# A cross-attention and maxout kernel: its opening re-ordered, and its two PSUM pools joined into one ring

## The chip, the cores and the metric

The kernel runs on one core of one Trainium2 chip. The metric is the device time of one execution in microseconds (us). The kernel before takes 152.98 us, the median of three runs (152.91 to 153.26). The profiled execution took 152.91 us by that measure; its trace spans 151.1 us from the first to the last instruction, so a time is about 1.8 us more than the span of its trace. The granted TensorE clock is 1.00 throughout.

Engines are named as the profile names them: PE is TensorE (PEld its weight loads), DVE is VectorE, ACT is ScalarE, POOL is GpSimd, and SP is the engine that issues the DMAs.

## The reference

Eight batches of 8 heads. Tokens `x` (512 per batch and head, 64 wide) and a small `state` (32 rows per head) attend to each other; both reads then go, as rows of 512 features, through a maxout layer.

```python
# B, H, S, Ns, D = 8, 8, 512, 32, 64
scores = scale * x @ state^T ;   a  = softmax(scores)     # over the 32 states
xread  = a @ state                                        # 512 rows per head
scores2 = scale * state @ x^T ;  a2 = softmax(scores2)    # over the 512 tokens
sread  = a2 @ x                                           # 32 rows per head
rows   = concat([xread, sread])                           # (8*544, 512)
out    = max(rows @ w1, rows @ w2) @ w_out                # w1, w2: 512x1024, w_out: 1024x512
```

Inputs and output are float32. The kernel works in bf16 on PE and rests on an identity: max(h1, h2) = h2 + relu(h1 - h2), so out = relu(rows @ (w1 - w2)) @ w_out + rows @ (w2 @ w_out). The weight W = [w1 - w2 | w2 @ w_out], 512 x 1536, is called `wcat`. For the x rows, a @ (state @ W) is used in place of (a @ state) @ W: `SW[b]` is state times W for batch b, in three column parts (0 and 1 for the relu, 2 for the direct part).

## The kernel before

The program is one hand-ordered list: each engine runs its own instructions in the order of the text. First the loads are issued on one DMA queue:

```python
load_states(first)                  # states of batches 0 to 2
load_x(0, 2)                        # x of batch 0, in two DMAs (even heads, odd heads)
for ch in range(2):
    load_w(w2f, moe_w2, ch)         # half of w2, 1 MB
    load_wo(2 * ch); load_wo(2 * ch + 1)   # two quarters of w_out, 0.5 MB each
load_w(w1f, moe_w1, 0)
load_x(1)
load_w(w1f, moe_w1, 1)
load_states(slice(3, 8))
load_x(2)
```

The pieces that both versions are made of (cut):

```python
def d_xt(b):        # x of a batch, transposed by a DMA from the bf16 copy xc
    nc.sync.dma_start_transpose(out=st[b]["xt"], in_=st[b]["xc"]...)
def u_exp(b, g):    # scores of half the heads (16 small matmuls in all for g = 0, 1), then exp on ACT
def u_norm(b, g, mul):   # row sums and reciprocal on DVE, then a = e * er on the engine `mul`
def u_sr(b):        # state read: 32 small matmuls, then reciprocal and scaling on DVE
def u_at(b, eng):   # a transposed by PE (8 transposes), copied out by `eng`
def compact_x(b, g, eng="A"):   # half of x cast to bf16 into xc
def w_sub(q, eng=nc.gpsimd):    # a quarter of w1 - w2 into wcat
    eng.tensor_sub(wcat[:, :, cs], w1f[:, :, cs], w2f[:, :, cs])
def w_wo(q, i): ... # w2 @ w_out, 2 of the 8 terms of row block i

def sw_mm(b, ch, engs="VA"):        # SW[b], column part ch, 8 matmuls on two PSUM banks
    pg = [bank(kind="acc" if ch == 2 and b > 1 else "ps") for g in range(2)]
    two = b < TWO and ch == 0       # from w1 and -w2 apart (16 matmuls), as wcat isn't there yet
    terms = ((sbd, w1b), (sneg, w2b)) if two else ((sbd, wcat),)
    ...                             # copied out: one bank by DVE, one by ACT

def l1(b, fill, fs=range(NF), engs=None):    # 8 blocks of 2 matmuls and a relu, ACT and DVE in turn
def l2_open(b, c): ...   # 2 matmuls of the direct part open the sum of output block c (4 blocks)
def l2_add(b, c, fs):    # one matmul for each f in fs onto the sum of block c
def l2_close(b, c): ...  # copied out by DVE (c even) or ACT (c odd)
```

PSUM has eight banks, four in a pool `ps` and four in a pool `acc`. The opening, from the second half of w_out on:

```python
    ...                                   # x(0) transposed, scored; w2 transposed; w2 @ w_out begun
    for e, i in (("V", slice(0, 2)), ("A", slice(2, 3)), ("P", slice(3, 4))):
        copy(e, w1b[:, i, 0:512], w1f[:, i, 0:512])       # first half of w1 to bf16, three engines
    for i in range(4):
        w_wo(3, i)
    w_wo_out(0); w_wo_out(1)
    u_sw(0, 0)
    w_wo_out(2); w_wo_out(3)
    compact_x(1, 0, "P"); compact_x(1, 1, "P")
    d_xt(1)
    l1(0, {2: [lambda: u_sw(0, 2)]}, range(0, 4))
    cast_x(1, (("A", slice(0, 4)), ("A", slice(4, 8))))
    load_x(3)
    w_sub(2, nc.vector); w_sub(3, nc.vector)
    cast_states("P", rest)
    sT = d_states(rest)
    for c in range(NC):
        l2_open(0, c)
    for c in range(NC - 1):
        l2_add(0, c, range(0, 4))
    u_sw(0, 1)
    l2_add(0, 3, range(0, 4))
    u_exp(1, 0); u_exp(1, 1)              # needs xt(1)
    l1(0, {}, range(4, 8))
    u_norm(1, 0, nc.vector); u_norm(1, 1, nc.gpsimd)
    cast_x(2)
    w_sub(0); w_sub(1)
    l2_add(0, 0, range(4, 8)); l2_close(0, 0)
    u_sw(1, 1)
    u_sr(1)
    l2_add(0, 1, range(4, 8)); l2_close(0, 1)
    u_sw(1, 0)
    compact_x(2, 0); compact_x(2, 1)
    d_xt(2)
    l2_add(0, 2, range(4, 8)); l2_close(0, 2)
    u_at(1, "V")
    u_sw(1, 2)
    u_srt(1)
    l2_add(0, 3, range(4, 8)); l2_close(0, 3)
    l2_out(0)
    for b in range(1, B):                 # the main loop, seven batches
        fill = fillers(b)                 # the next batch's scores, state read, DMAs and SW, set
        ...                               # between the blocks of l1(b) and l2(b)
        l1(b, fill)
        if b == B - 1:
            moe_sread()                   # the state rows through the maxout layer
        l2(b, fill)
```

Of the kernel before, what the change touches and what calls it, by code (L numbers as in the profile page):

```python
# [9 lines left out]
BF16 = mybir.dt.bfloat16  # L10
# [5 lines left out]
def kernel(  # L16
# [14 lines left out]
    nc = tc.nc  # L31
# [4 lines left out]
    FF = moe_w1.shape[1]  # L36
# [11 lines left out]
    keep = ctx.enter_context(tc.tile_pool(name="keep", bufs=2))  # L48
    big = ctx.enter_context(tc.tile_pool(name="big", bufs=2))

    pools = {k: ctx.enter_context(tc.tile_pool(name=k, bufs=4, space=bass.MemoryType.PSUM)) for k in ("ps", "acc")}
    ctx.enter_context(tc.manual_schedule())

    def bank(dtype=F32, kind="ps"):
        return pools[kind].tile([128, 512 if dtype == F32 else 1024], dtype, tag="b", name=kind)

    def acc():
        return bank(kind="acc")

    def copy(eng, o, i):  # L60
        if eng == "A":
            nc.scalar.copy(o, i)  # L62
        elif eng == "V":
            nc.vector.tensor_copy(o, i)  # L64
        else:
            nc.gpsimd.tensor_copy(o, i)  # L66
# [11 lines left out]
    def load_x(b, parts=1):  # L78
        xf_t[b] = xio.tile([128, H, NC * D], F32, tag="xf", name="xf")
        for g in range(parts):  # L80
            nc.sync.dma_start(out=xf_t[b][:, g::parts, :], in_=x[b, g::parts].rearrange("h (p c) d -> p h (c d)", c=NC))  # L81
# [12 lines left out]
    def load_w(t, w, ch):  # L94
        cs = slice(ch * 512, (ch + 1) * 512)
        nc.sync.dma_start(out=t[:, :, cs], in_=w.rearrange("(i p) f -> p i f", p=128)[:, :, cs])  # L96
# [3 lines left out]
                          in_=moe_w_out.rearrange("(k p) n -> p k n", p=128)[:, 2 * q:2 * q + 2])  # L100

    load_states(first)
    load_x(0, 2)
    for ch in range(2):
        load_w(w2f, moe_w2, ch)
        load_wo(2 * ch)
        load_wo(2 * ch + 1)
    load_w(w1f, moe_w1, 0)
    load_x(1)
    load_w(w1f, moe_w1, 1)  # L110
    load_states(slice(3, 8))
    load_x(2)

# [6 lines left out]
    sneg = consts.tile([128, TWO, 4, Ns], BF16)  # L120
    wo = consts.tile([128, NF, DM], BF16)
    wcat = consts.tile([128, 4, WC], BF16)
    w1b = stage.tile([128, 4, 512], BF16)
    w2b = stage.tile([128, 4, FF], BF16)
    w2t = stage.tile([128, 4, NF, 128], BF16)

    def warm_up(n):
        p = bank()
        for k in range(n):
            nc.tensor.matmul(p, warm[:, 0:128], warm, start=(k == 0), stop=(k == n - 1))  # L130
# [28 lines left out]
    def negate_states():  # L159
        for g in range(2):  # L160
            gs = slice(64 * g, 64 * g + 64)
            negate("V", sneg[gs], sbd[gs, 0:TWO, g::2, g, :])
# [11 lines left out]
    def cast_x(b, parts=(("P", slice(0, 8)),)):  # L174
        new_x(b)
        xp = st[b]["xp"] = xio.tile([128, H, NC, 66], BF16, tag="xp", name="xp")
        nc.gpsimd.memset(xp[:, :, :, 64:65], 1.0)
        for e, hs in parts:
            copy(e, xp[:, hs, :, 0:64], xf_t[b][:, hs].rearrange("p h (c d) -> p h c d", c=NC))
# [40 lines left out]
    def u_norm(b, g, mul):  # L220
        d = st[b]
        nc.vector.tensor_reduce(d["es"][:, g], d["e"][:, g].rearrange("p i c n -> p (i c) n"),  # L222
                                axis=mybir.AxisListType.X, op=ALU.add)
        nc.vector.reciprocal(d["er"][:, g], d["es"][:, g])  # L224
        mul.tensor_mul(  # L225
            d["a"][:, g].rearrange("p c i n -> p i c n"), d["e"][:, g],
            d["er"][:, g].rearrange("p (i c) -> p i c", i=4).unsqueeze(3).to_broadcast([128, 4, NC, Ns]))
# [22 lines left out]
    def u_at(b, eng):  # L250
        d = st[b]
        AT[b] = keep.tile([128, 2, NC * 128], BF16, tag="at", name="aT")
        p = bank(BF16)
        for g in range(2):
            for c in range(NC):
                nc.tensor.transpose(p[:, (g * NC + c) * 128:(g * NC + c + 1) * 128],
                                    d["a"][:, g, c].rearrange("p i n -> p (i n)"), ident)
        copy(eng, AT[b].rearrange("p g t -> p (g t)"), p)
# [8 lines left out]
    swt = consts.tile([128, 2, 2, WC], BF16)  # L267

    def sw_mm(b, ch, engs="VA"):

        pg = [bank(kind="acc" if ch == 2 and b > 1 else "ps") for g in range(2)]
        two = b < TWO and ch == 0
        terms = ((sbd, w1b), (sneg, w2b)) if two else ((sbd, wcat),)
        for k, (sv, w) in enumerate(terms):
            for i in range(4):
                for g in range(2):
                    gs = slice(64 * g, 64 * g + 64)
                    nc.tensor.matmul(pg[g][32 * i:32 * i + 32, :],  # L278
                                     sneg[gs, b, i, :] if k else sbd[gs, b, 2 * i + g, g, :],
                                     w[gs, i, ch * 512:(ch + 1) * 512],  # L280
                                     start=(k == 0), stop=(k == len(terms) - 1))
        return lambda: [copy(engs[g], SW[b][:, g, ch * 512:(ch + 1) * 512], pg[g]) for g in range(2)]
# [96 lines left out]
                nc.sync.dma_start(out=out[b * L + S:(b + 1) * L], in_=ob[32 * q:32 * q + 32, t, :])  # L379


    def w_sub(q, eng=nc.gpsimd):
        cs = slice(q * 256, (q + 1) * 256)
        eng.tensor_sub(wcat[:, :, cs], w1f[:, :, cs], w2f[:, :, cs])

    def w_cast(o, w, ch, engs="VA"):
        cs = slice(ch * 512, (ch + 1) * 512)
        for k in range(2):
            copy(engs[k], o[:, 2 * k:2 * k + 2, cs], w[:, 2 * k:2 * k + 2, cs])
# [4 lines left out]
    def w_t(ch, half, eng):  # L394
        p = bank(BF16)
        for j in range(2):
            for k in range(4):
                f = 4 * ch + k
                nc.tensor.transpose(p[:, (4 * j + k) * 128:(4 * j + k + 1) * 128],
                                    w2b[:, 2 * half + j, f * 128:(f + 1) * 128], ident)  # L400
        copy(eng, w2t[:, 2 * half:2 * half + 2, 4 * ch:4 * ch + 4, :].rearrange("p j f t -> p j (f t)"),
             p.rearrange("p (j t) -> p j t", j=2))
# [3 lines left out]
    def w_wo(q, i):  # L406
        if q == 0:
            WO[i] = acc()
        for f in range(2 * q, 2 * q + 2):
            nc.tensor.matmul(WO[i], w2t[:, i, f, :], wo[:, f, :], start=(f == 0), stop=(f == NF - 1))  # L410

    def w_wo_out(i):
        copy("V" if i % 2 else "A", wcat[:, i, FF:WC], WO[i])


    def fillers(b):
# [22 lines left out]
    warm_up(6)  # L439
    cast_states("V", first)  # L440
    states(first)
    warm_up(9)
    cast_x(0, (("A", slice(0, 4, 2)), ("V", slice(4, 8, 2)), ("P", slice(1, 4, 2)), ("V", slice(5, 8, 2))))
    u_xt(0, 0, "V")
    warm_up(2)
    u_xt(0, 1, "A")
    u_exp(0, 0)
    warm_up(2)
    u_exp(0, 1)
    warm_up(3)  # L450
    w_cast(w2b, w2f, 0, "PA")
    u_norm(0, 0, nc.vector)
    u_norm(0, 1, nc.vector)
    w_t(0, 0, "A")
    w_t(0, 1, "A")
    u_sr(0)
    wo_cast(0, "P")
    wo_cast(1, "P")
    warm_up(1)
    for i in range(4):  # L460
        w_wo(0, i)
    u_at(0, "V")
    w_cast(w2b, w2f, 1)
    for i in range(4):
        w_wo(1, i)
    w_t(1, 0, "V")
    w_t(1, 1, "A")
    negate_states()
    wo_cast(2, "P")
    wo_cast(3, "P")  # L470
    u_srt(0)
    warm_up(2)
    for i in range(4):
        w_wo(2, i)
    for e, i in (("V", slice(0, 2)), ("A", slice(2, 3)), ("P", slice(3, 4))):
        copy(e, w1b[:, i, 0:512], w1f[:, i, 0:512])
    for i in range(4):
        w_wo(3, i)
    w_wo_out(0)
    w_wo_out(1)  # L480
    u_sw(0, 0)
    w_wo_out(2)
    w_wo_out(3)
    compact_x(1, 0, "P")
    compact_x(1, 1, "P")
    d_xt(1)
    l1(0, {2: [lambda: u_sw(0, 2)]}, range(0, 4))
    cast_x(1, (("A", slice(0, 4)), ("A", slice(4, 8))))
    load_x(3)
    w_sub(2, nc.vector)  # L490
    w_sub(3, nc.vector)
    cast_states("P", rest)
    sT = d_states(rest)
    for c in range(NC):
        l2_open(0, c)
    for c in range(NC - 1):
        l2_add(0, c, range(0, 4))
    u_sw(0, 1)
    l2_add(0, 3, range(0, 4))
    u_exp(1, 0)  # L500
    u_exp(1, 1)
    l1(0, {}, range(4, 8))
    u_norm(1, 0, nc.vector)
    u_norm(1, 1, nc.gpsimd)
    cast_x(2)
    w_sub(0)
    w_sub(1)
    l2_add(0, 0, range(4, 8))
    l2_close(0, 0)
    u_sw(1, 1)  # L510
    u_sr(1)
    l2_add(0, 1, range(4, 8))
    l2_close(0, 1)
    u_sw(1, 0)
    compact_x(2, 0)
    compact_x(2, 1)
    d_xt(2)
    l2_add(0, 2, range(4, 8))
    l2_close(0, 2)
    u_at(1, "V")  # L520
    u_sw(1, 2)
    u_srt(1)
    l2_add(0, 3, range(4, 8))
    l2_close(0, 3)
    l2_out(0)
    for b in range(1, B):
        fill = fillers(b)
        if b + 2 < B:
            cast_x(b + 2)
            if b + 3 < B:  # L530
                load_x(b + 3)
        if b == 1:
            fill[11].append(lambda: put_states(rest, sT))
        l1(b, fill)
        if b == B - 1:
            moe_sread()
        l2(b, fill)
# [30 lines left out]
```

## Time and profile before

| What | Value |
|---|---|
| Time, median of three | 152.98 us |
| Span of the trace | 151.1 us |
| Instructions | 3008 |
| Matmul 128x512 of the output sums (L321), mean | 379 ns each as recorded, issued one each 0.216 us |
| DMA, whole span | 29.89 MB, mean 198 GB/s |
| HBM read, written | 15.20 MB, 8.91 MB |

The trace has three parts. The opening reaches from the start to the first matmul of the main loop, which stands at 42.77 us on the timeline. The main loop then takes one batch after the other. The end holds the state rows and the last batch's output. In a view of the timeline a row gives the start in us, the busy time in us, the engine, the line of the program, the operation, the tile written and the tiles read, the shape, and how many instructions are merged in the row; in brackets is the idle time of the engine ahead of it and what ended it. Line 64 is the copy of DVE, line 62 that of ACT and line 66 that of POOL, so these are told apart by their tiles. In the chain of waits a row gives a start, a length, and what filled it.

### The profile page before, as it was taken

What the parts mean: (1) busy time and instruction counts of PE and PEld (TensorE: products, weight loads), DVE (VectorE), ACT (ScalarE), POOL (GpSimd) and SP (SyncE); (2) the same over time, 40 slices, a digit from 0 to 9 for tenths busy, and PEclk for the clock granted to TensorE, in tenths of its full rate; (3) what the DMA queues carried; (4) which work ended last, traced back from release to release, by engine and by line L of the source; (5) the groups of instructions that cost most, each with busy time, mean ns of one, the idle gap of its engine ahead of it and who ended that gap; (6) DMA issues with size and microseconds to landing.
All of it is one profiled execution on the core that took longest, in us unless ns stands there. A gap on an engine that the chain in (4) does not pass through costs nothing.

```text
span 151.1 us, 3008 instructions
## 1 busy us (share of the span) xinstructions
PE 140.4 (93%) x1237; PEld 67.3 (45%) x1257; DVE 82.7 (55%) x149; ACT 74.8 (49%) x126; POOL 42.9 (28%) x46
## 2 busy tenths in 40 slices
PE   6979897979999999999999999999999999999991
PEld 1445542424444434544543454345445444664460
DVE  5548636815987367806762584558167726631120
ACT  3166536615888347815863684469157126621010
POOL 3145255410599540370054007303200500000000
PEclk9999999999999999999999999999999999999999
DMA  4999999999269995975888397952496030602423
GB/s 100 382 385 387 386 359 348 319 143 288 52 117 306 313 177 195 295 168 112 262 293 167 95 292 241 165 193 104 86 129 278 0 74 22 256 0 68 138 98 119
DMA packets 37950, 29.89 MB, mean 198 GB/s; under 512 B 24880, under 2 KB 33328, under 8 KB 37040
## 3 DMA queue, kind: packets, MB, share of 16 engines
q1 hardware_dynamic: 37792, 29.56, 70.7%
q8 instruction: 10, 0.16, 0.4%
q10 hardware_dynamic: 144, 0.13, 0.3%
q14 instruction: 4, 0.03, 0.1%
HBM read 15.20 MB, written 8.91 MB: 160 GB/s over the span
## 4 chain that ended last, share of the span: by engine, by line
PE 68%; DMA 13%; SPq 11%; DVE 4%; issue 1%; ACT 0%
PE acc L321 31%; PE ps L306 15%; PE acc L317 8%; DMA xt<-xc 7%; SPq L96 7%; DMA s_f<-in_state_dram 6%; PE ps L215 2%; SPq L81 2%; PE ps L365 2%; PE acc L375 2%; PE ps L278 2%; SPq L99 2%; PE ps L238 1%; PE acc L355 1%; PE acc L373 1%
## 5 line engine op out<-in xcount | busy, mean ns | idle before, releaser
L321 PE MATMUL acc<-wo,r 128*128 128x512 bf16 x239 | 58.5, 379 | 0.7 <-issue 0.2
L321 PEld LDWEIGHTS <-r 128*128 128x128 bf16 x248 | 24.0, 98 | 29.6 <-issue 0.6
L296 DVE TENSOR_SCALAR r<-ps 128x512 bf16<-128x512 f32 x32 | 22.1, 691 | 15.6 <-PE ps L306 15.6
L306 PE MATMUL ps<-aT,swt 128*128 128x512 bf16 x127 | 29.2, 379 | 0.9 <-DVE swt L64 0.8
L225 POOL TENSOR_TENSOR a<-e,er 128x512 bf16<-128x512 bf16 x13 | 13.4, 1048 | 55.5 <-DVE er L224 28.3
L64 DVE COPY ob<-acc 128x512 f32<-128x512 f32 (+1 forms) x17 | 11.1, 652 | 30.2 <-PE acc L321 29.8
L62 ACT COPY ob<-acc 128x512 f32<-128x512 f32 (+1 forms) x16 | 9.2, 573 | 28.5 <-PE acc L321 20.9
L294 ACT ACTIVATE r<-ps 128x512 bf16<-128x512 f32 x32 | 19.2, 601 | 5.2 <-PE ps L306 4.5
L306 PEld LDWEIGHTS <-swt 128*128 128x128 bf16 x128 | 12.1, 98 | 15.4 <-DVE swt L64 1.2
L62 ACT CAST swt<-ps 128x512 bf16<-128x512 f32 x18 | 10.0, 587 | 17.1 <-PE ps L278 17.1
L317 PE MATMUL acc<-swt,aT 128*128 128x512 bf16 x56 | 16.7, 380 | 1.2 <-issue 1.0
L66 POOL CAST xp<-xf 128x2048 bf16<-128x2048 f32 (+1 forms) x7 | 12.2, 1743 | 9.3 <-DMA xf<-in_x_dram 9.3
L64 DVE CAST swt<-ps 128x512 bf16<-128x512 f32 x18 | 11.8, 682 | 2.6 <-PE ps L278 2.5
L222 DVE TENSOR_REDUCE es<-e 128x16 f32<-128x512 bf16 x16 | 10.6, 662 | 3.7 <-ACT e L218 3.7
L62 ACT CAST xc<-xf 128x1024 bf16<-128x1024 f32 x12 | 12.0, 1051 | 0.0
L218 ACT ACTIVATE e<-ps 128x512 bf16<-128x512 f32 x16 | 8.8, 595 | 2.9 <-PE ps L215 2.2
L130 PE MATMUL ps<-warm 128*128 128x512 bf16 x24 | 7.6, 443 | 1.3 <-POOL warm L116 1.3
L410 PE MATMUL acc<-wo,w2t 128*128 128x512 bf16 x30 | 7.3, 379 | 0.5 <-POOL wo L66 0.4
L317 PEld LDWEIGHTS <-aT 128*128 128x128 bf16 x62 | 4.7, 98 | 6.4 <-issue 3.1
L215 PE MATMUL ps<-sbd,xt 128*128 128x64 bf16 x128 | 5.2, 193 | 1.8 <-DMA xt<-xc 1.1
L215 PEld LDWEIGHTS <-xt 128*128 128x128 bf16 x128 | 4.6, 98 | 4.3 <-DMA xt<-xc 2.2
L66 POOL CAST wo<-wof 128x1024 bf16<-128x1024 f32 x4 | 4.3, 1066 | 4.9 <-DMA wof<-in_moe_w_out_dram 4.9
(74 smaller groups left out, 120.7 us busy)
## 6 DMA issues: line engine op xcount, KB each, us to landing
xf<-in_x_dram SPq DMA_DIRECT2D x7, 1024.0 KB, 7.6
out_dram<-ob SPq DMA_DIRECT2D x7, 1024.0 KB, 5.0
w2f<-in_moe_w_dram SPq DMA_DIRECT2D x2, 1024.0 KB, 9.3
wof<-in_moe_w_out_dram SPq DMA_DIRECT2D x4, 512.0 KB, 11.0
w1f<-in_moe_w_dram SPq DMA_DIRECT2D x2, 1024.0 KB, 15.3
xf<-in_x_dram SPq DMA_DIRECT2D x2, 512.0 KB, 4.8
out_dram<-ob SPq DMA_DIRECT2D x3, 256.0 KB, 2.4
out_dram<-obs SPq DMA_DIRECT2D x8, 64.0 KB, 1.7
```

The costliest lines, as they stand in the source:

```text
L62: nc.scalar.copy(o, i)
L64: nc.vector.tensor_copy(o, i)
L66: nc.gpsimd.tensor_copy(o, i)
L96: nc.sync.dma_start(out=t[:, :, cs], in_=w.rearrange("(i p) f -> p i f", p=128)[:, :, cs])
L215: nc.tensor.matmul(p[:, k * 64:k * 64 + 64], d["xt"][:, 4 * i + 2 * g + cp, :], sbd[:, b, 2 * i + g].rearrange("p u n -> p (u n)"), start= ...
L222: nc.vector.tensor_reduce(d["es"][:, g], d["e"][:, g].rearrange("p i c n -> p (i c) n"), axis=mybir.AxisListType.X, op=ALU.add)
L225: mul.tensor_mul(d["a"][:, g].rearrange("p c i n -> p i c n"), d["e"][:, g], d["er"][:, g].rearrange("p (i c) -> p i c", i=4).unsqueeze(3) ...
L294: nc.scalar.activation(out=o, in_=p, func=ACTF.Relu)
L296: nc.vector.tensor_scalar(o, p, scalar1=0.0, scalar2=None, op0=ALU.max)
L306: nc.tensor.matmul(p, SW[b][:, g, f * 128:(f + 1) * 128], AT[b][:, g, :], start=(g == 0), stop=(g == 1))
L317: nc.tensor.matmul(OB[b][1 + c], AT[b][:, g, c * 128:(c + 1) * 128], SW[b][:, g, FF:WC], start=(g == 0), stop=False)
L321: nc.tensor.matmul(OB[b][1 + c], R[b][:, f, c * 128:(c + 1) * 128], wo[:, f, :], start=False, stop=(f == NF - 1))
```

## The change

The change rewrites the opening and how PSUM is shared; the filler schedule and the main loop are the same text in both. What it does:

- The loads: x(0) comes in one DMA, and both halves of w1 come before x(1).
- Fewer warm-up matmuls (15 in place of 24), and other engines for several casts: both casts of the first half of w2 on DVE, the last quarter of w_out on DVE, the halves of w1 on DVE and ACT alone.
- The second half of w1 gets a bf16 copy too, so that three parts of SW come from w1 and w2 apart: (0,0), (0,1) and (1,1), where before they were (0,0) and (1,0). No w1 - w2 is needed from DVE: all four quarters of `w_sub` run on POOL, two of them early.
- The bf16 copy of x(1) for its transposing DMA is made by ACT, later in the order, and the cast of x(1) for the state read is made by POOL.
- The scores of batch 1 come after the second half of l1(0), not before it. Several parts of SW and the last transposes change places.
- At the end of the opening the two PSUM pools are closed, and the main loop takes all banks from one ring of eight. What it is for: each block can then have any bank, and the relu of a block has more time before its bank is wanted again.

```diff
-    pools = {k: ctx.enter_context(tc.tile_pool(name=k, bufs=4, space=bass.MemoryType.PSUM)) for k in ("ps", "acc")}
+    early = ctx.enter_context(ExitStack())
+    pools = dict(ps=early.enter_context(tc.tile_pool(name="ps", bufs=4, ...)), acc=...)   # cut
+    def one_ring():
+        early.close()
+        pools["ps"] = pools["acc"] = ctx.enter_context(tc.tile_pool(name="ring", bufs=8, space=bass.MemoryType.PSUM))
...
-    load_x(0, 2)
+    load_x(0)
...
     load_w(w1f, moe_w1, 0)
+    load_w(w1f, moe_w1, 1)
     load_x(1)
-    load_w(w1f, moe_w1, 1)
...
-        pg = [bank(kind="acc" if ch == 2 and b > 1 else "ps") for g in range(2)]
-        two = b < TWO and ch == 0
+        pg = [bank(), bank()]
+        two = b < TWO and ch < 2 and (b, ch) != (1, 0)
...
-    w_cast(w2b, w2f, 0, "PA")
+    w_cast(w2b, w2f, 0, "VV")
...
-    for e, i in (("V", slice(0, 2)), ("A", slice(2, 3)), ("P", slice(3, 4))):
-        copy(e, w1b[:, i, 0:512], w1f[:, i, 0:512])
+    wo_cast(3, "V")
+    ...
+    w_cast(w1b, w1f, 0)
+    w_sub(0)
+    w_sub(1)
     for i in range(4):
         w_wo(3, i)          # after: copied out block by block inside
     u_sw(0, 0)
-    compact_x(1, 0, "P")
-    compact_x(1, 1, "P")
-    d_xt(1)
-    l1(0, {2: [lambda: u_sw(0, 2)]}, range(0, 4))
-    cast_x(1, (("A", slice(0, 4)), ("A", slice(4, 8))))
-    load_x(3)
-    w_sub(2, nc.vector)
-    w_sub(3, nc.vector)
-    cast_states("P", rest)
-    sT = d_states(rest)
+    u_sw(0, 2)
+    l1(0, {}, range(0, 4))
     for c in range(NC):
         l2_open(0, c)
-    for c in range(NC - 1):
-        l2_add(0, c, range(0, 4))
+    w_cast(w1b, w1f, 1)
+    compact_x(1, 0)
+    compact_x(1, 1)
+    d_xt(1)
+    cast_x(1)
+    w_sub(2)
+    w_sub(3)
+    cast_states("P", rest)
+    load_x(3)
+    sT = d_states(rest)
+    l2_add(0, 0, range(0, 4))
     u_sw(0, 1)
-    l2_add(0, 3, range(0, 4))
-    u_exp(1, 0)
-    u_exp(1, 1)
+    for c in range(1, NC):
+        l2_add(0, c, range(0, 4))
     l1(0, {}, range(4, 8))
-    u_norm(1, 0, nc.vector)
-    u_norm(1, 1, nc.gpsimd)
+    u_sc(1, 0, nc.vector)       # u_exp and u_norm
+    u_sc(1, 1, nc.gpsimd)
     cast_x(2)
-    w_sub(0)
-    w_sub(1)
     l2_add(0, 0, range(4, 8))
     l2_close(0, 0)
-    u_sw(1, 1)
-    u_sr(1)
+    u_sw(1, 0)
     l2_add(0, 1, range(4, 8))
     l2_close(0, 1)
-    u_sw(1, 0)
+    u_sw(1, 1)
+    u_sr(1)
     compact_x(2, 0)
     compact_x(2, 1)
-    d_xt(2)
     l2_add(0, 2, range(4, 8))
     l2_close(0, 2)
     u_at(1, "V")
-    u_sw(1, 2)
-    u_srt(1)
     l2_add(0, 3, range(4, 8))
     l2_close(0, 3)
+    d_xt(2)
+    u_sw(1, 2)
+    u_srt(1)
     l2_out(0)
+    one_ring()
     for b in range(1, B):
```

More of the change, by code (lines that the diff above doesn't have):

```diff
@@ L49 @@
     big = ctx.enter_context(tc.tile_pool(name="big", bufs=2))
-    pools = {k: ctx.enter_context(tc.tile_pool(name=k, bufs=4, space=bass.MemoryType.PSUM)) for k in ("ps", "acc")}
+    early = ctx.enter_context(ExitStack())
+    pools = dict(ps=early.enter_context(tc.tile_pool(name="ps", bufs=4, space=bass.MemoryType.PSUM)),
+                 acc=early.enter_context(tc.tile_pool(name="acc", bufs=4, space=bass.MemoryType.PSUM)))
     ctx.enter_context(tc.manual_schedule())
@@ L122 @@
     wcat = consts.tile([128, 4, WC], BF16)
-    w1b = stage.tile([128, 4, 512], BF16)
+    w1b = stage.tile([128, 4, FF], BF16)
     w2b = stage.tile([128, 4, FF], BF16)
@@ L379, in moe_sread, with w_sub @@
                 nc.sync.dma_start(out=out[b * L + S:(b + 1) * L], in_=ob[32 * q:32 * q + 32, t, :])
-    def w_sub(q, eng=nc.gpsimd):
+    def w_sub(q):
         cs = slice(q * 256, (q + 1) * 256)
-        eng.tensor_sub(wcat[:, :, cs], w1f[:, :, cs], w2f[:, :, cs])
+        nc.gpsimd.tensor_sub(wcat[:, :, cs], w1f[:, :, cs], w2f[:, :, cs])
     def w_cast(o, w, ch, engs="VA"):
@@ L410, in w_wo @@
             nc.tensor.matmul(WO[i], w2t[:, i, f, :], wo[:, f, :], start=(f == 0), stop=(f == NF - 1))
-    def w_wo_out(i):
-        copy("V" if i % 2 else "A", wcat[:, i, FF:WC], WO[i])
+        if q == 3:
+            copy("V" if i % 2 else "A", wcat[:, i, FF:WC], WO[i])
     def fillers(b):
@@ L441 @@
     states(first)
-    warm_up(9)
-    cast_x(0, (("A", slice(0, 4, 2)), ("V", slice(4, 8, 2)), ("P", slice(1, 4, 2)), ("V", slice(5, 8, 2))))
+    warm_up(5)
+    cast_x(0, (("V", slice(0, 4, 2)), ("A", slice(4, 8, 2)), ("V", slice(1, 4, 2)), ("P", slice(5, 8, 2))))
     u_xt(0, 0, "V")
-    warm_up(2)
     u_xt(0, 1, "A")
     u_exp(0, 0)
-    warm_up(2)
     u_exp(0, 1)
-    warm_up(3)
-    w_cast(w2b, w2f, 0, "PA")
[L452 to L456, printed above, removed]
+    w_cast(w2b, w2f, 0, "VV")
     wo_cast(0, "P")
@@ L459 @@
     warm_up(1)
-    for i in range(4):
-        w_wo(0, i)
-    u_at(0, "V")
+    w_t(0, 0, "A")
+    w_t(0, 1, "A")
+    u_norm(0, 0, nc.vector)
+    u_sr(0)
+    u_norm(0, 1, nc.vector)
+    negate_states()
+    warm_up(3)
+    for q in range(2):
+        for i in range(4):
+            w_wo(q, i)
     w_cast(w2b, w2f, 1)
-    for i in range(4):
-        w_wo(1, i)
+    wo_cast(2, "P")
     w_t(1, 0, "V")
     w_t(1, 1, "A")
-    negate_states()
-    wo_cast(2, "P")
-    wo_cast(3, "P")
+    u_at(0, "V")
     u_srt(0)
-    warm_up(2)
+    wo_cast(3, "V")
     for i in range(4):
         w_wo(2, i)
-    for e, i in (("V", slice(0, 2)), ("A", slice(2, 3)), ("P", slice(3, 4))):
-        copy(e, w1b[:, i, 0:512], w1f[:, i, 0:512])
+    w_cast(w1b, w1f, 0)
+    w_sub(0)
+    w_sub(1)
     for i in range(4):
         w_wo(3, i)
-    w_wo_out(0)
-    w_wo_out(1)
     u_sw(0, 0)
-    w_wo_out(2)
-    w_wo_out(3)
-    compact_x(1, 0, "P")
-    compact_x(1, 1, "P")
-    d_xt(1)
-    l1(0, {2: [lambda: u_sw(0, 2)]}, range(0, 4))
-    cast_x(1, (("A", slice(0, 4)), ("A", slice(4, 8))))
-    load_x(3)
-    w_sub(2, nc.vector)
-    w_sub(3, nc.vector)
-    cast_states("P", rest)
-    sT = d_states(rest)
+    u_sw(0, 2)
+    l1(0, {}, range(0, 4))
     for c in range(NC):
         l2_open(0, c)
-    for c in range(NC - 1):
+    w_cast(w1b, w1f, 1)
[9 more added lines that the diff above has]
+    l2_add(0, 0, range(0, 4))
+    u_sw(0, 1)
+    for c in range(1, NC):
         l2_add(0, c, range(0, 4))
-    u_sw(0, 1)
-    l2_add(0, 3, range(0, 4))
-    u_exp(1, 0)
-    u_exp(1, 1)
     l1(0, {}, range(4, 8))
-    u_norm(1, 0, nc.vector)
-    u_norm(1, 1, nc.gpsimd)
+    u_sc(1, 0, nc.vector)
+    u_sc(1, 1, nc.gpsimd)
     cast_x(2)
-    w_sub(0)
-    w_sub(1)
     l2_add(0, 0, range(4, 8))
     l2_close(0, 0)
+    u_sw(1, 0)
+    l2_add(0, 1, range(4, 8))
+    l2_close(0, 1)
     u_sw(1, 1)
     u_sr(1)
-    l2_add(0, 1, range(4, 8))
-    l2_close(0, 1)
-    u_sw(1, 0)
     compact_x(2, 0)
     compact_x(2, 1)
-    d_xt(2)
     l2_add(0, 2, range(4, 8))
@@ L520 @@
     u_at(1, "V")
+    l2_add(0, 3, range(4, 8))
+    l2_close(0, 3)
+    d_xt(2)
     u_sw(1, 2)
     u_srt(1)
-    l2_add(0, 3, range(4, 8))
-    l2_close(0, 3)
     l2_out(0)
+    one_ring()
     for b in range(1, B):
```

## The prediction

> **What bounds the kernel now.** I read the page first, then the chain of waits in order of time, then the timeline of the first 60 us, because the diff touches only the opening. The page:
>
> ```profile
> PE 140.4 (93%) x1237; PEld 67.3 (45%) x1257; DVE 82.7 (55%) x149; ACT 74.8 (49%) x126; POOL 42.9 (28%) x46
> PE   6979897979999999999999999999999999999991
> ```
>
> PE is busy 93% of the span, and the 40 slices (3.78 us each) show where the missing 7% lies: slices below 9 stand only among the first nine, so up to 34 us, and in the last. After that PE alone sets the time. The chain of waits says the same with times:
>
> ```profile
> 26.76 7.00 DMA xt<-xc
> ...
> 33.81 0.64 PE ps L215 x16
> 34.45 1.74 PE ps L306 x8
> ...
> 36.90 0.60 DVE es L222
> ...
> 42.12 0.06 DVE aT L64
> 42.18 4.26 DMA xt<-xc
> ...
> 57.17 3.45 PE ps L306 x16
> ...
> 71.13 3.45 PE ps L306 x16
> ```
>
> The main loop runs from 57.17 to 71.13, 13.96 us a batch, all PE: 56 matmuls of 0.216 us are 12.1, and scores, state read and SW are the rest. The ring can hardly shorten that. The opening is another matter: up to 26.76 the chain is DMA issue and loads, then the transposing DMA of x(1) lands at 33.76, then a chain on DVE (36.8 to 42.7) releases l1(1). So the prediction is one number, the time at which the first matmul of l1(1) starts; it was 42.77. The rows I take it from, of the timeline:
>
> ```profile
> 11.24 1.04 POOL L66 CAST wo<-wof 128x1024 bf16<-128x1024 f32 x1 [0.33 <-DMA wof<-in_moe_w_out_dram]
> 11.31 1.50 DVE L225 TENSOR_TENSOR a<-e,er 128x512 bf16<-128x512 bf16 x1
> ...
> 21.68 0.69 DVE L64 CAST w1b<-w1f 128x1024 bf16<-128x1024 f32 x1 [2.53 <-DMA w1f<-in_moe_w_dram]
> 21.71 1.14 POOL L66 CAST w1b<-w1f 128x512 bf16<-128x512 f32 x1 [1.66 <-DMA w1f<-in_moe_w_dram]
> ...
> 36.82 0.67 DVE L222 TENSOR_REDUCE es<-e 128x16 f32<-128x512 bf16 x1
> ...
> 42.44 4.67 POOL L384 TENSOR_TENSOR wcat<-w1f,w2f 128x1024 bf16<-128x1024 f32 x2
> 42.64 0.68 DVE L64 CAST swt<-ps 128x512 bf16<-128x512 f32 x1
> 42.77 3.61 PE L306 MATMUL ps<-aT,swt 128*128 128x512 bf16 x15
> ```
>
> [...] at 11.31 DVE's product took 1.50 us beside POOL's cast, while the other products took 0.69; at 21.71 POOL's 128x512 cast took 1.14 us, longer than the 1.04 of a 128x1024 one, as if it waited out DVE's 0.69. [...] the first six warm-up matmuls take 2.74 us, the nine at 4.54 take 2.11. [...] xt(1), issued at 26.76 behind x(2), needs 7.00 us to land; xt(2), with nothing ahead, 4.26.
>
> **The change part by part.**
>
> *Until the first half of w1.* x(0) is one DMA, so its first cast moves from 5.64 to about 7.15 and the softmax of batch 0 follows about 1 us later. I walked it through: scores at 9.3 and 10.2, exps to 11.4, w2's first half cast on DVE 9.9 to 11.25, w2t copies on ACT to 13.4, a(0) complete at 15.0, sneg at 16.0, w2's second half at 16.7 (it ended at 16.67 before). So the delay is swallowed by the wait for loads: the last quarter of w_out lands at 19.0 and w1's first half at 21.68 in both. w_wo(3) ends near 22.4 in both. Nine warm-ups fewer are PE work nobody waits for.
>
> *w1 and SW(0).* DVE and ACT each cast half of w1's first half: 21.68 to 22.37 and to 22.73. POOL's w_sub(0) wakes by the same load[...]. SW(0,0) ends near 23.5, as before; then SW(0,2), l1's first four blocks 24.5 to 26.2, l2_open to 28.0. In the kernel before l2_open ended at 28.8, as SW(0,2) stood inside l1.
>
> *The second half of w1.* It lands near 24.6, x(1) near 27.5 (they change places; each took about 3 us). POOL: w_sub(0) and (1) at 2.35 each from 22.4 to 27.1. DVE's cast comes after its last relu, 27.0, [...] and ends at 27.8. ACT's part ends at 27.5. SW(0,1), now 16 matmuls in place of 8 (+0.4), runs 28.9 to 29.7; the remaining 12 of l2_add to 32.3; l1's second half to 34.05.
>
> *xt(1).* ACT starts the compact copies when x(1) is in: 27.5 plus 2 x 1.05 is 29.6. Then d_xt(1). It finds x(2) nearly landed, so about 4.3 us as for xt(2): 33.9. It landed at 33.76 before. So the scores start at about 34.1, as before (33.81); but the 1.74 us of l1's second half, which stood after them, are already done. This is the gain.
>
> *The DVE chain.* Exp ends at 35.2, so the first row sum starts there and not at 36.82: 1.6 us sooner. From that row sum to the last SW copy DVE has the same twelve instructions, which took from 36.82 to 43.32, 6.5 us. POOL is late: it does cast_x(1) to 29.7, w_sub(2) and (3) to 34.4, the states' cast (2.0) to 36.4. DVE's product at 36.1 waits for that, +0.3. So the last copy ends near 42.1.
>
> *The ring.* In the program as built, the first matmul of l1(1) now waits for the last copy of DVE (SW(1,2)) and the last of ACT (sread_t), as the old pools are closed; before, it needed only aT, at 42.72, one DVE copy (0.68) earlier. So this eats 0.6 of the 1.6. ACT: the second half of l2_add(0,3) ends at 40.7, then ob 0.6, swt 0.6, sread_t 0.3, so 42.2.
>
> l1(1) then starts near 42.3, a gain of 0.5. In the loop the ring offers each block a bank freed eight allocations ago; counting 22 allocations per batch I find no bank wanted before its reader is done. So 13.96 a batch stays. The end is the same. w_sub off POOL at 42.44 to 47.1 may save part of the 0.28 by which the first batch (42.77 to 57.01) exceeds 13.96. Nominal: 152.98 - 0.5 - 0.1 = 152.4.
>
> **The rivals.** What can go wrong is all on one side, as each is a wait which the kernel before doesn't have.
>
> [...] Then w1's cast on DVE waits 2.35 us behind w_sub(0), and SW(0,0), l1 and all after it come 2 us later: 154.4. For: both wake on the same load, 30 ns apart. Against: DVE was first at 21.68 and with x(0). One in four.
>
> [...] If DVE's cast of w1's second half isn't served between w_sub(1) and cast_x(1), it waits 1.9 more and SW(0,1) comes about 1.2 late: 153.6. One in four. The same at 36.1, with three POOL instructions back to back, is worth up to 0.7.
>
> *xt(1) late.* Three casts and ACT's compact copies precede it, x(1) lands a megabyte later, and x(2) may not be out of the queue; with the 7.0 us of before it lands at 36.6, and all is 2.5 late: 154.9. For: the window of 30 to 34 us moved few bytes at full DMA busyness. Against: the bytes ahead of it are the same in both. I take 1 us late at two in five.
>
> *A cold PE.* Between the warm-ups and the first transposes PE idles about 1.9 us, with light work to 13 us. If the clock halves there, w_wo(0) and (1) take about 1.3 us more: 153.7. One in four.
>
> *The ring shortens the loop.* Were l1 waiting for banks, 0.1 a batch would give 0.7. Against: 16 matmuls of l1 take 3.45, back to back already.
>
> **Range and chances.** Weighted, the rivals add 0.25 x 2.0 + 0.25 x 1.2 + 0.4 x 1.0 + 0.25 x 1.3 = 1.5, and some of them hide one another; I take 1.1. So 153.5. Low end: none comes true and the chain is 0.4 quicker, 152.0. High end: two come true, 155.8. Faster by 2% would be under 149.9, which needs 3 us out of an opening whose loads set most of it: 0.02. Slower by 2% is over 156.0, two large rivals together: 0.10. Within 2%: 0.88.
>
> **What would show it.** The first L306 matmul of l1(1) near 42.3 to 43.5, after SW(1,2)'s copy and not aT's; the scores of batch 1 at about 34, straight behind l1(0)'s last block; the cast of w1 on DVE at 21.7 taking 0.69 [...]; d_xt(1) issued near 29.6 and landing by 34; warm-ups and w_wo at 0.216 us each; 13.96 us from one l1 to the next. If the loop's period changes, or the first 22 us cost PE time, the prediction is wrong in kind.

## The result, and the profile after

The changed kernel takes 152.01 us (median of four runs, 151.89 to 155.04; a run that is disturbed like this last one is left out of the ratios, here and below) against 153.04 for the kernel before in the same job. The ratio is 0.9929, with a 95% interval of 0.9909 to 0.9948: 1.0 us faster, clear of the noise and well within 2%. The prediction had 153.5, so slower by 0.5. Its sign was wrong.

The page of the kernel after shows that the loop is as it was, and that the granted clock of PE fell in the opening:

```profile
PE 140.0 (93%) x1235; PEld 68.3 (45%) x1255; DVE 82.3 (55%) x151; ACT 75.6 (50%) x126; POOL 43.9 (29%) x44
PE   6769999999889999999999999999999999999990
PEclk9977999999999999999999999999999999999999
```

The two sevens in the clock stand at 7.5 to 15 us (0.77, and 0.50 from 9.8 to 12.6); the kernel before has nines throughout (its first six warm-ups took 2.74 us, where nine later ones took 2.11, and the record of the clock doesn't show this). PE is filled from slice 12 on, as before. The chain of waits after, with start, length and what filled it:

```profile
27.87 1.99 ACT xc L68 x2
29.86 0.03 ACT swt L68
29.89 4.36 DMA xt<-xc
...
34.74 0.61 ACT e L224
...
35.37 0.70 DVE es L228
...
40.65 0.58 ACT ob L68
41.23 0.49 ACT swt L68
41.72 0.18 ACT sread_t L68
41.90 0.04 issue
41.94 3.62 PE ps L311 x16
45.56 0.47 PE ps L221 x16
...
70.03 3.45 PE ps L311 x16
83.99 3.45 PE ps L311 x16
```

Three things are to be read here. The scores of batch 1 still wait for the transposed x(1), which lands at 34.25 (33.76 before). But the first row sum of DVE starts at 35.37, not at 36.82, as nothing stands between the scores and the exp any more. And the last link ahead of l1(1) (L311) is no longer aT on DVE but `sread_t`, the last copy of ACT: without the ring the link is aT again, as the first experiment shows. l1(1) starts at 41.94 in place of 42.77, a gain of 0.83. The loop then keeps its period, 83.99 - 70.03 = 13.96 us.

Between l1(1) and l1(3) another 0.27 is gained: 70.03 - 41.94 = 28.09, where before it was 71.13 - 42.77 = 28.36. In the kernel before l1(1) started at 42.77, but the scores of batch 2 only at 46.49, the time at which the transposed x(2) landed; here they follow l1(1) at once (45.40 in the timeline). The chain of the kernel before has the row:

```profile
46.49 0.64 PE ps L215 x16
```

Together this is 1.10 of trace, of which 1.0 is seen in the time.

The rows of the timeline after that answer to those shown of before, at the two places where DVE and POOL meet and at the start of l1(1):

```profile
22.15 0.69 DVE L70 CAST w1b<-w1f 128x1024 bf16<-128x1024 f32 x1 [1.75 <-DMA w1f<-in_moe_w_dram]
22.21 5.17 POOL L389 TENSOR_TENSOR wcat<-w1f,w2f 128x1024 bf16<-128x1024 f32 x2 [3.04 <-DMA w1f<-in_moe_w_dram]
...
27.24 0.85 DVE L70 CAST w1b<-w1f 128x1024 bf16<-128x1024 f32 x1
...
36.38 0.69 DVE L231 TENSOR_TENSOR a<-e,er 128x512 bf16<-128x512 bf16 x1
...
41.20 0.68 DVE L70 CAST swt<-ps 128x512 bf16<-128x512 f32 x1
41.60 0.28 ACT L68 COPY sread_t<-ps 128x128 bf16<-128x128 bf16 x1
41.94 3.62 PE L311 MATMUL ps<-aT,swt 128*128 128x512 bf16 x16 [0.83 <-ACT sread_t L68]
```

At 22.15 DVE's cast took 0.69, and it was POOL that took longer: its two subtractions took 5.17 where two took 4.67 before. At 27.24 DVE's cast took 0.85, 0.16 more than the one at 22.15; at 36.38 its product took 0.69. The last row holds the price of the ring: PE is idle 0.83 us for `sread_t`, where without the ring it is idle 0.22 for aT (first experiment).

### The profile page after: what moved, and what is told of

The parts are those of the page before. It is cut to its first block, busy times and chain, and to the rows that moved or that the text cites. A ratio compares the mean times of both kernels' runs of the same rounds, so it can differ in the third digit from the quotient of the medians.

```text
span 150.1 us, 3012 instructions
## 1 busy us (share of the span) xinstructions
PE 140.0 (93%) x1235; PEld 68.3 (45%) x1255; DVE 82.3 (55%) x151; ACT 75.6 (50%) x126; POOL 43.9 (29%) x44
## 2 busy tenths in 40 slices
DMA packets 37934, 29.89 MB, mean 199 GB/s; under 512 B 24864, under 2 KB 33312, under 8 KB 37024
## 4 chain that ended last, share of the span: by engine, by line
PE 70%; DMA 13%; SPq 7%; ACT 3%; DVE 2%; issue 1%
PE acc L326 31%; PE ps L311 16%; DMA xf<-in_x_dram 10%; PE acc L322 8%; SPq L102 4%; SPq L105 3%; PE ps L283 3%; DMA xt<-xc 3%; PE ps L370 2%; PE acc L380 2%; PE ps L221 2%; PE ps L244 1%; PE acc L360 1%; ACT xc L68 1%; PE acc L378 1%
## 5 line engine op out<-in xcount | busy, mean ns | idle before, releaser
L326 PE MATMUL acc<-wo,r 128*128 128x512 bf16 x238 | 57.8, 379 | 0.6 <-issue 0.2
L311 PE MATMUL ps<-aT,swt 128*128 128x512 bf16 x127 | 29.0, 379 | 1.0 <-ACT sread_t L68 0.8
L70 DVE COPY ob<-acc 128x512 f32<-128x512 f32 (+1 forms) x17 | 11.1, 653 | 30.2 <-PE acc L326 29.8
L68 ACT CAST swt<-ps 128x512 bf16<-128x512 f32 x24 | 12.9, 593 | 12.3 <-PE ps L283 12.2
L311 PEld LDWEIGHTS <-swt 128*128 128x128 bf16 x128 | 12.1, 98 | 15.3 <-DVE swt L70 1.3
L72 POOL CAST xp<-xf 128x2048 bf16<-128x2048 f32 (+1 forms) x8 | 14.1, 1768 | 10.2 <-DMA xf<-in_x_dram 10.2
L70 DVE CAST swt<-ps 128x512 bf16<-128x512 f32 x24 | 15.3, 681 | 1.8 <-PE ps L283 1.7
L68 ACT CAST xc<-xf 128x1024 bf16<-128x1024 f32 x14 | 13.9, 1051 | 0.1
L389 POOL TENSOR_TENSOR wcat<-w1f,w2f 128x1024 bf16<-128x1024 f32 x4 | 9.8, 2473 | 3.0 <-DMA w1f<-in_moe_w_dram 3.0
L136 PE MATMUL ps<-warm 128*128 128x512 bf16 x14 | 6.0, 568 | 1.5 <-POOL warm L122 1.3
L283 PE MATMUL ps<-wcat,sbd 64*32 64x512 bf16 x168 | 6.7, 380 | 0.1
```

What stands on the lines that cost most here:

```text
L283: nc.tensor.matmul(pg[g][32 * i:32 * i + 32, :], sneg[gs, b, i, :] if k else sbd[gs, b, 2 * i + g, g, :], w[gs, i, ch * 512:(ch + 1) * 512 ...
L311: nc.tensor.matmul(p, SW[b][:, g, f * 128:(f + 1) * 128], AT[b][:, g, :], start=(g == 0), stop=(g == 1))
L326: nc.tensor.matmul(OB[b][1 + c], R[b][:, f, c * 128:(c + 1) * 128], wo[:, f, :], start=False, stop=(f == NF - 1))
L389: nc.gpsimd.tensor_sub(wcat[:, :, cs], w1f[:, :, cs], w2f[:, :, cs])
```

## The experiments

Theory A: the gain comes from the place of the scores in PE's order. With the second half of l1(0) ahead of them, PE works while x(1) is being transposed, and the DVE chain starts sooner. The ring costs a wait at l1(1). Rival B: the ring brings the gain. Rival C: the place of the scores alone does nothing; the casts and subtractions on other engines are needed. Each time stands beside the kernel before on the same chip; its medians were 153.14 in the first job, 153.15 in the second and 153.18 in the third. In the expectations e3 is the kernel before with the scores late, e4 the changed kernel with the scores early, and e9 the kernel before with x(2) compacted on POOL.

### The changed kernel without the ring

```diff
-        pg = [bank(), bank()]
+        pg = [bank(kind="acc" if ch == 2 and b > 1 else "ps") for g in range(2)]
...
-    one_ring()
```

> The changed kernel without the one ring: the pools ps and acc stay for the main loop, with part 2 of SW taken from acc there as before. Theory A (the opening brings the gain, the ring costs a wait at l1(1)): l1(1) starts when aT is copied, near 41.35 in place of 41.94, so 0.6 us less than the changed kernel, about 151.4. Rival B (the ring brings the gain): the gain is gone, 152.9 or more. If the ring does neither: 152.0.

Measured: 151.55 us, ratio 0.9896 (0.9879 to 0.9913), so 1.59 less than before where the changed kernel was 1.03 less. The ring costs 0.56 by these medians, 0.50 by the ratios, and 0.53 by the start of l1(1) (41.94 and 41.41); rival B falls, and the loop's period is 13.96 here too. In its chain of waits aT on DVE is the last link again:

```profile
40.76 0.61 DVE aT L70
41.37 0.04 issue
41.41 3.62 PE ps L311 x16
45.03 0.47 PE ps L221 x16
```

### The kernel before with the ring

```diff
+        early.close()
+        pools["ps"] = pools["acc"] = ctx.enter_context(tc.tile_pool(name="ring", bufs=8, ...))
...
     l2_out(0)
+    one_ring()
```

> The kernel before, with the pools closed and one ring of eight for the main loop. Theory A: l1(1) waits for the last copies of DVE and ACT, near 43.4 in place of 42.77, and of that 0.27 is won back as the transposed x(2) is then no longer waited for: 153.4, or 0.3 to 0.4 slower. Rival B: 152.0 to 152.3.

Measured: 153.53 us, ratio 1.0027 (1.0015 to 1.0040): 0.39 slower, as expected. Its chain of waits runs through one more copy, the cast of SW(1,2):

```profile
42.34 0.60 DVE aT L70
42.93 0.61 DVE swt L70
43.54 0.04 issue
43.59 3.63 PE ps L312 x16
```

The wait for the new pool is 0.6; part comes back, as the transposed x(2) has landed by the time that it is wanted.

### The kernel before with the scores late, and nothing else

```diff
-    u_exp(1, 0)
-    u_exp(1, 1)
     l1(0, {}, range(4, 8))
+    u_exp(1, 0)
+    u_exp(1, 1)
```

> The kernel before, with the scores of batch 1 behind the second half of l1(0) and nothing else changed. Theory A (PE does the 1.74 us of l1 while x(1) is still being transposed, and the DVE chain starts 1.4 us sooner): l1(1) near 41.4, but the transposed x(2) may then be waited for by 0.5, so 151.5 to 152.0. Rival C (the gain needs the casts and w_sub on other engines as well): within 0.3 of 153.0.

Measured: 151.50 us, ratio 0.9895 (0.9878 to 0.9911). Two lines moved bring 1.64, more than the whole change, and rival C falls. The chain of waits:

```profile
32.72 1.74 PE ps L306 x8
34.47 0.25 PE ps L215 x8
...
35.37 0.70 DVE es L222
...
40.63 4.43 DMA xt<-xc
45.06 0.05 issue
45.10 0.64 PE ps L215 x16
```

PE comes from l1 straight into the scores at 34.3. The row sum starts at 35.37, as in the changed kernel. What is left is the transposed x(2): l1(1) starts at 41.33 in the timeline, its 3.45 us end at 44.8, and the scores of batch 2 start at 45.10.

### The changed kernel with the scores early

```diff
+    u_exp(1, 0)
+    u_exp(1, 1)
     l1(0, {}, range(4, 8))
-    u_sc(1, 0, nc.vector)
-    u_sc(1, 1, nc.gpsimd)
+    u_norm(1, 0, nc.vector)
+    u_norm(1, 1, nc.gpsimd)
```

> The changed kernel, with the scores of batch 1 ahead of the second half of l1(0), as before, and nothing else changed. Theory A: PE stands from 32.3 until the transposed x(1) lands at 34.25, then l1's half runs, and the first row sum starts near 37.3 in place of 35.37: about 2 us slower than the changed kernel, 153.5 to 154.0. Rival C: within 0.3 of 152.0.

Measured: 154.68 us, ratio 1.0115 (1.0061 to 1.0168), so 2.6 more than the changed kernel relative to before, and more than theory A said. The stretches of its trace (length, PE busy and number of matmuls, granted clock, DMA share, GB/s) show what the excess is:

```profile
32.00:34.00 2.00, 0.00 (x0) 1.00 0.91 201
34.00:36.00 2.00, 1.63 (x20) 0.84 0.89 227
36.00:38.00 2.00, 2.00 (x6) 0.50 1.38 338
38.00:40.00 2.00, 2.00 (x14) 0.80 0.76 119
```

PE stands still for 2.5 us, up to 34.37. Its clock is 0.50 from 36 to 38; by an estimate from the means of the stretches beside it (0.84 and 0.80) it is so from 35.4 to 38.8. The eight matmuls of l1 take 2.95 us in place of 1.74.

### The same, with PE kept warm in the gap

```diff
+    warm_up(8)
     u_exp(1, 0)
     u_exp(1, 1)
```

> e4 (the changed kernel with its scores early) with eight warm-up matmuls in PE's gap of 2.5 us ahead of the scores. In e4 the clock fell to 0.50 at 36 to 38 us and the eight matmuls of l1 took 2.95 us in place of 1.74. If that cold stretch is the part of e4's loss that I hadn't expected: 1.2 less than e4, 153.3 to 153.6. If not: 154.5.

Measured: 154.12 us, ratio 1.0053 (1.0032 to 1.0075), 0.94 over before. l1's eight matmuls take 1.89 as the timeline records them, where the row of the one with the gap was 3.09, and the row sum starts at 37.62 in place of 38.59. The scores started at 34.61 here and at 34.37 there, so from the scores to the row sum it is 3.01 in place of 4.22: in these two traces the cold stretch cost 1.2, as expected. By the medians it was worth 0.6 (1.54 over before, now 0.94), by the ratios 0.95, with four runs of each kernel. Two of those with the gap were at 154.25, close to the warmed kernel; one of the two has a mean clock of 1.00, so the clock didn't fall in each execution (the other, at 0.975, stays unexplained). What remains is the order: 1.97 over the changed kernel relative to before by the medians, 1.9 by the ratios, where 2.0 was expected.

### x(0) in two DMAs again

```diff
-    load_x(0)
+    load_x(0, 2)
```

> The changed kernel with x(0) loaded in two DMAs again, nothing else. All loads of the changed kernel land later than before, the first half of w1 at 22.15 in place of 21.68. If the one DMA causes that: w1 lands near 21.7, x(1) near 27.4, the transposed x(1) near 33.8, and the time falls by 0.4, to 151.6. If the order of w1 and x(1), or chance, causes it: within 0.15 of the changed kernel, 152.0.

Measured: 152.00 us, ratio 0.9923 (0.9903 to 0.9943): no difference to the changed kernel. The first half of w1 is cast at 21.90 and not 22.15, but the same cast stands between 21.57 and 22.25 in the traces of this study, whichever way x(0) is loaded, so this shows nothing of the loads. In this trace the load 0.25 sooner was not worth its time: PE waited 0.42 for the transposed x(1), which landed as late as in the changed kernel.

### The warm-ups put back

```diff
-    warm_up(5)
+    warm_up(9)
...
     u_xt(0, 0, "V")
+    warm_up(2)
     u_xt(0, 1, "A")
     u_exp(0, 0)
+    warm_up(2)
     u_exp(0, 1)
+    warm_up(3)
```

> The changed kernel with the warm-up matmuls of before put back (9 after the states, 2, 2 and 3 around the scores). The granted clock was 0.77 from 7.5 to 15 us of the changed kernel and 1.00 before. Theory (the loads hide the cold stretch): the clock is 1.00 there, w_wo starts sooner, and the time is the same, 151.8 to 152.1. Rival (the cold PE delays w_wo(3) and with it SW(0,0)): 0.3 to 0.8 less.

Measured: 152.18 us, ratio 0.9934 (0.9920 to 0.9949), the same as the changed kernel. Its clock is 1.00 from 4 to 19 us. In the changed kernel the two stretches between 7.5 and 15 us read:

```profile
7.50:11.30 3.80, 2.66 (x49) 0.77 1.05 392
11.30:15.00 3.70, 3.54 (x56) 0.77 1.05 386
```

So the clock fell with the fewer warm-ups (0.77, where it is 1.00 with them), and in this trace that cost nothing: w_wo(3) ended at 22.82, just ahead of w1's cast at 22.84. The same opening wasn't as lucky in another trace. In that of the kernel with PE kept warm in the gap, whose program is the same up to that gap, the two stretches and the start of SW(0,0) read:

```profile
7.50:11.30 3.80, 2.67 (x49) 0.64 1.05 395
11.30:15.00 3.70, 3.70 (x56) 0.50 1.05 386
...
22.07 0.69 DVE L70 CAST w1b<-w1f 128x1024 bf16<-128x1024 f32 x1 [0.41 <-DMA w1f<-in_moe_w_dram]
23.78 0.41 PE L283 MATMUL ps<-w1b,sbd 64*32 64x512 bf16 x8
```

There PE was at w_wo(3) until 23.85 and took up SW(0,0) 1.0 after w1's cast had ended (22.76); d_xt(1) was issued at 30.18 in place of 29.89. So the cold opening cost some 0.3 at that step in this trace; the medians (152.18 with the warm-ups, 152.01 without) don't show it.

### POOL first at w1

```diff
+    nc.vector.tensor_copy(first_look, w1f[:, 0, 0:1])
     w_cast(w1b, w1f, 0)
     w_sub(0)
```

> The changed kernel with a copy of one column on DVE ahead of the cast of w1, so that POOL's w_sub(0) begins first. [...] DVE's cast ends about 2.4 later (near 25.2 in place of 22.84), SW(0,0) and l1(0) follow, and the scores of batch 1 come 2 us later: 153.8 to 154.4. If the two share: within 0.3 of 152.0.

Measured: 152.47 us, ratio 0.9954 (0.9939 to 0.9968), 20 runs from 151.81 to 155.27, and inconclusive. The copy of one column took 0.15 and the cast's row begins 0.07 after the start of the copy's, at 22.24, and 0.01 after that of POOL; it took 0.68, so POOL's subtraction didn't delay it, though its row began first. So the delay was made longer, by a row sum that takes 0.69:

```diff
+    nc.vector.tensor_reduce(first_look, w1f[:, 0, 0:512], axis=mybir.AxisListType.X, op=ALU.add)
     w_cast(w1b, w1f, 0)
```

> The changed kernel with a row sum over 512 columns of w1 on DVE (about 0.6 us, an operation that showed no contention) ahead of its cast of w1, so that POOL's w_sub(0) is under way [...]. [...] the cast ends near 25.2 in place of 22.84, and the time is 153.5 to 154.4. If only the added 0.6 us counts: 152.4 to 152.7, as some of it is hidden by the wait for the transposed x(1).

Measured: 155.44 us, ratio 1.0111 (1.0079 to 1.0143), runs from 153.41 to 155.81. Now the cast is delayed; the timeline:

```profile
22.10 0.69 DVE L476 TENSOR_REDUCE first_look<-w1f 128x1 f32<-128x512 f32 x1 [2.02 <-DMA w1f<-in_moe_w_dram]
22.16 5.11 POOL L390 TENSOR_TENSOR wcat<-w1f,w2f 128x1024 bf16<-128x1024 f32 x2 [3.05 <-DMA w1f<-in_moe_w_dram]
22.71 2.35 DVE L70 CAST w1b<-w1f 128x1024 bf16<-128x1024 f32 x1
...
25.11 0.41 PE L284 MATMUL ps<-w1b,sbd 64*32 64x512 bf16 x8 [2.34 <-DVE w1b L70]
...
26.91 3.53 PE L312 MATMUL ps<-aT,swt 128*128 128x512 bf16 x8 [0.21 <-DVE swt L70]
```

The row sum ran beside POOL and took 0.69, as row sums of 128x512 do elsewhere in these traces (0.67 to 0.69); the cast, beside POOL's subtractions, took 2.35 in place of 0.69 and ended at 25.06 in place of 22.84. This is 2.2, some 0.6 of it the row sum's own time and 1.7 the longer cast; the rival, without a row sum, had a wait of 2.35. The time rose by more: by 3.3 relative to before by the medians (1.03 under, now 2.26 over), by 2.8 by the ratios, with a wide spread between runs. In the trace PE was idle for 2.34, its clock was 0.52 from 26.9 to 30.2, and l1's first eight matmuls took 3.53 where 1.89 stood before.

### Further than both

In the kernel before with late scores two things stood in the way: x(2), and the DVE chain. First the compact copies of x(2) go to POOL, which has nothing to do from 31 to 38 us, with the transposing DMA right behind them; then DVE's two copies of output blocks go to ACT, which is freed by that.

```diff
     u_exp(1, 1)                       # late, as above
+    compact_x(2, 0, "P")
+    compact_x(2, 1, "P")
...
     w_sub(1)
+    d_xt(2)
...
-    compact_x(2, 0)
-    compact_x(2, 1)
-    d_xt(2)
```

> The kernel before with the scores of batch 1 late (as in e3) and the compact copies of x(2) on POOL in its idle time, ahead of the product, with their transposing DMA right after. e3 still waited 0.3 for the transposed x(2) and for aT by DVE. Theory: the wait for x(2) goes, the DVE chain stays: 151.1 to 151.3. [...] nothing is gained: 151.5 to 152.

Measured: 151.54 us, ratio 0.9898 (0.9883 to 0.9913), no better than the late scores alone. The wait for x(2) is gone (scores at 44.98, which is l1(1)'s 41.53 and 3.45), but w1 landed 0.2 later in this trace, so the 0.3 can't be told from the noise. The expectation's other outcome, 151.5 to 152, supposed that POOL's copies would delay DVE's product at 36.4. In the trace of the next kernel, which has the same copies, they ended at 36.11 and the product, at 36.26, took 0.69.

```diff
-    copy("A" if c % 2 else "V", ob[:, c, :], OB[b][1 + c])
+    copy("A" if c % 2 or b == 0 else "V", ob[:, c, :], OB[b][1 + c])
```

> e9 with the first batch's output blocks 0 and 2 copied out by ACT in place of DVE: two copies of 0.6 fewer in the DVE chain between the first row sum and aT. If that chain still sets l1(1): 1.0 less than e9, 150.5. If PE is the next bound: from the end of the scores (34.9) it has 6.2 us of matmuls left before l1(1), so l1(1) near 41.2 and 151.1 to 151.4. If ACT, now with both, becomes the bound: 151.5 or more.

Measured: 150.77 us, ratio 0.9851 (0.9833 to 0.9869), 2.4 less than the kernel before and the fastest of all. Its timeline:

```profile
39.52 0.69 DVE L64 COPY aT<-ps 128x1024 bf16<-128x1024 bf16 x1
...
39.82 1.03 PE L321 MATMUL acc<-wo,r 128*128 128x512 bf16 x4
...
40.69 3.62 PE L306 MATMUL ps<-aT,swt 128*128 128x512 bf16 x16
```

aT is ready at 40.2, but PE is still at the last sums (39.82 to 40.85 as recorded) and goes from them into l1(1). Now PE is the bound, as it is in the loop. I had expected 41.2 for that. By the chain of waits PE's work from the end of the scores (34.81) to the end of the last sums (40.85) is 6.04, where I had counted 6.2. Part of the step from e9's trace, where l1(1) stands at 41.53, is that w1's cast came 0.32 sooner here; the ratios of the two runs differ by 0.7 us.

## Why the prediction was wrong, point by point

- **Which stage decides, and the loop's period.** Right. The ring left 13.96 as it was.
- **The opening up to w1.** The order of events was right, and x(0)'s first cast, w_wo(3) and w1's cast came 0.35 to 0.5 later than worked out (7.50, 22.82 and 22.15 for 7.15, 22.4 and 21.68). For w1's cast this is within the spread of the traces, 21.57 to 22.25.
- **The scores ahead or behind l1(0).** Right, and the heart of the matter: DVE's chain started at 35.37 for a predicted 35.2. Moved alone it brings 1.64 (kernel before) or 1.97 (kernel after, warmed).
- **xt(1).** Predicted 33.9, landed 34.25: this rival came true by a third of its size. The 4.3 us for its DMA was an estimate from xt(2)'s 4.26; it took 4.36.
- **The ring.** The wait was named with its two copies. Put at 0.6, it is 0.56 here and 0.39 on the kernel before.
- **l1(1).** The nominal 42.3 against 41.94. DVE's last copy ended at 41.88 (42.1 predicted): the chain has thirteen instructions, not twelve, and took 6.51, as counted; the product on DVE wasn't held up by the states' cast, which took 1.25 of POOL and not 2.0, so the term of 0.3 for POOL was 0 (the product took 0.69). ACT's last copy ended at 41.88 too and not at 42.2: its three copies took 1.23 together, where the sum of their rows had given 1.5.
- **The first batch of the loop.** The 0.28 was put to w_sub on POOL and counted as 0.1. It was the wait for the transposed x(2): before with late scores it was still there; with x(2) compacted on POOL it went, while w_sub stayed where it was. In the changed kernel d_xt(2) is issued at 40.26 and not at 42.18.
- **The step that failed: what the rivals were added for.** The mechanism and the nominal sum held: 152.4 is within 0.4 of the result and on the right side. Then the prediction added 1.1 for four rivals and so turned a gain of 0.6 into a loss of 0.5. In the changed kernel's trace the four cost next to nothing. POOL did not go first (w1's cast on DVE took 0.69). At 27 the cast took 0.16 longer. The transposed x(1) came 0.35 later than worked out, in place of 1.0. The cold PE occurred (a clock of 0.77 from 7.5 to 15 us) and cost nothing, for a price of 1.3; in another execution it cost some 0.3. That DVE would wait for POOL was an estimate, for which the trace of before had DVE's product at 11.31 (1.50 in place of 0.69); for the cast only the kernel with the row sum shows it (2.35 in place of 0.69). That the clock would halve after 1.9 us of idleness wasn't shown by the trace of before, whose clock is 1.00 throughout. In spite of these delays l1(1) started 0.36 ahead of the nominal 42.3. The prediction's own reasoning could have priced the cold PE lower, as it says that a delay there is swallowed by the wait for loads. POOL first was priced at 2.0 and cost 2.8 to 3.3 when it was made to happen, the row sum included; the price was no exaggeration. DVE's cast took 0.68 or 0.69 in all seven traces in which both engines were woken by the same load for these operations (the one with the copy of one column among them); at one in four this would still happen about one time in eight, so the chance isn't refuted.

So 1.03 can be told as steps between kernels that were run: 1.64 less for the place of the scores (kernel before with the scores late), 0.05 more for the rest of the new opening (changed kernel without the ring; no difference by the noise), 0.56 more for the ring. Taken the other way round, from the changed kernel, the place of the scores is worth some 2.0, so the parts don't simply add; which part of the new opening makes it worth more there wasn't tried.

## What to carry to other kernels

In a hand-ordered stream like this one, work that waits for nothing belongs ahead of work that waits for a transfer; here two lines in that order were worth 1.64, more than the whole change (1.03). Closing the two memory pools and opening another was a wait for the last readers of the old buffers, here 0.4 to 0.6 us, so do it where an engine waits anyway. And when each step of a prediction has been followed to a number, risks that the reasoning itself has found to be covered should widen the range, not move its middle.

## What the runs showed that I had not expected

- The PE clock fell to half after gaps that I hadn't counted on. After gaps of 2.51 us (the changed kernel with the scores early) and 2.34 us (the one with the row sum) the clock was 0.50 from 36 to 38 and 0.52 from 26.9 to 30.2. By an estimate from the mean clocks of the stretches, the half clock reached from 35.4 to 38.8 and from 27.0 to 30.4: it began 1.0 and 1.9 us after PE had resumed work and lasted 3.4 us. A gap of 1.41 in the changed kernel, up to 7.98, was followed by 0.50 from 9.8 to 12.6; one of 1.11 in the kernel before, up to 33.81, by 1.00 from 34 to 36.
- The gap on PE so cost twice: with POOL first, 2.2 us of delay at w1 became 3.6 us at the first row sum in the trace (38.97 for 35.37), and 2.8 to 3.3 us of time.
- The row that starts first is not always the one that isn't delayed: with the copy of one column POOL's row began at 22.23, 0.01 ahead of DVE's, yet DVE's cast took 0.68 and POOL's two subtractions 5.23, where two took 4.67 in the kernel before.
